# The newer form of attention units from the eighth unit on, with the raw weight tiles in a ring

## The chip, the cores and the metric

The kernel runs on one core of a Trainium2 chip. The metric is the device time of one execution in microseconds (us). Lower is better.

## The reference

A gated linear recurrence over 4 batches, 8 heads, 768 tokens and 48 channels feeds a mixture of 4 experts over 3072 rows of 384. All is float32.

```python
def _attn_ref(q, k, v, alpha):
    state = np.zeros((B, H, D, D)); y = np.zeros_like(q)
    for t in range(S):
        state = alpha[:, :, t, :, None] * state + np.einsum('bhd,bhe->bhde', k[:, :, t], v[:, :, t])
        y[:, :, t] = np.einsum('bhd,bhde->bhe', q[:, :, t], state)
    return y
def _moe_ref(x, domain_probs, w1, w2):       # x: 3072 x 384, w1: 4 x 384 x 1024, w2: 4 x 1024 x 384
    p = domain_probs / (domain_probs.sum(-1, keepdims=True) + 1e-09)
    out = np.zeros((N, D))
    for e in range(E):
        out += p[:, e:e + 1] * (np.maximum(x @ w1[e], 0.0) @ w2[e])
    return out
```

## The kernel before

**Units, groups and tasks.** The tokens are cut into 24 units: a unit `u` is one block of 128 tokens (`cb`, 0 to 5) of one batch (`b`, 0 to 3), with all 8 heads, counted from 0 with the batch running fastest. Units are put into groups `gi`: group 0 has units 0 and 1, group 1 units 2 to 5, group 2 units 6 to 9, and so on; the last has two. A task `(gi, e)` is expert `e` for the tokens of group `gi`: `up` makes 8 tiles of hidden values, each from 9 matmuls (L957, with weights and x split into a rounded part and a rest, three products for three chunks of the contraction) and `down` makes the four sums from 96 matmuls (L1023). ACT writes the rounded hidden value (L959), DVE the rest (`hidden_rest`, L979), both from the PSUM tile `one`. `one` and the sums `ops` share four PSUM banks (tag "g").

**Attention beside the matmuls.** The attention of a group is computed while an earlier group's tasks run: units 6 to 9 during the tasks (1, e), units 10 to 13 during (2, e). `deal` gives every step of a unit a due time on a nominal clock, and `advance` runs the steps that are due between two matmul blocks. So the order of instructions on each engine is fixed when the program is built. Each unit's step ends in a `yield`.

**The older form, `attention`.** DVE turns alpha, k and q into channel rows (L702), and makes the terms of a token with itself (L722, L723). Then for each of seven levels (1, 2, 4, up to 64 tokens) ACT copies q into a zero-padded block (`copy_q`, L756, two copies), DVE scales q and the decays (`next_q`, L763, L765) and the keys (`next_k`, L775, with a copy by ACT, L774). PE makes the scores of six levels as 48 matmuls (L782), with `far` for the seventh (L838), DVE takes them into `near` through masks (L792). The keys are turned on PE (L283, copied by ACT, L894), the results `yps` (L877) and the state terms `sps` (L904) follow.

**The newer form, `in_order`**, is used from unit `in_fours` on. The first two levels are replaced by terms of four tokens in rows: q and alpha are loaded by fours (eight DMAs, L184, into two tiles of raw weights, `four_tiles`, and three, L187, into `row_a`), POOL multiplies them (L492, L494), DVE multiplies by k and reduces (L504, L505). Only levels 2 to 5 are made on PE, as 32 matmuls, with `far`, all at one place (L578, L586). The keys are not turned on PE: DVE transposes them in blocks (L613), and they go to memory and back in another order (`over`, L622, and four DMAs, L629), so that `sps` is 16 small matmuls (L667). The `tail` of a unit (`yps`, L650, and `sps`) runs within the next unit's step. The times of its first 13 steps are HEAD_FIRST for the first such unit, HEAD_SECOND for the second, HEAD_EARLY and HEAD for all others; REST has the others. `load(u + 1, ...)` is issued from unit u's steps.

**Weights.** During group 0, raw float32 pieces of w1 and w2 come from the inputs into `raw` tiles (L232, L236); in the tasks (1, e), w2 still comes raw (four pieces for the next expert at the start of `down`), ACT and DVE split each piece (L250, L252), and POOL's queue stores the split piece to `kept` (L253). From then on pieces are read back from `kept` (L225). There are 12 `raw` tiles, in a pool that hands them out in turn; the newer form takes eight of them by `whole_raw` and by `xTs[LAST]` for its own data.

Of the kernel before, what the change touches and what calls it, by code (L numbers as in the profile page):

```python
# [10 lines left out]
F32 = mybir.dt.float32  # L11
F32R = mybir.dt.float32r
# [8 lines left out]
def kernel(  # L21
# [13 lines left out]
    B, H, S, D = q.shape  # L35
    E, DM, F = moe_w1.shape
    P = 128
    NCB = S // P
    NP = H // 2
# [3 lines left out]
    KC = DM // P  # L43
    FCH = F // P
    NT = B * P
    NQ = 4
    QF = F // NQ
    FPQ = FCH // NQ
    LEVELS = [1 << i for i in range(7)]
    HALF = P // 2  # L50
    FOUR = 4
# [90 lines left out]
    HEAD_SECOND = [0.02, 0.06, 0.1, 0.13, 0.16, 0.2, 0.25, 0.31, 0.37, 0.45, 0.52, 0.61, 0.66]  # L142
    REST = [0.05, 0.17, 0.3, 0.42, 0.58]
    in_runs = 2
    in_fours = half + 2 * B
    MARGIN = 6.0
    waiting = deque()
    clock = 0.0
# [7 lines left out]
    def load(u, names):  # L156
        if u >= len(units):
            return
        cb, b = units[u]
        for nm in names:  # L160
            src = srcs[nm][b, :, cb * P:(cb + 1) * P, :].rearrange("h s d -> s h d")
            if u == in_fours and nm == "q":
                nc.gpsimd.memset(row_a, 1.0)
            if u == in_runs and nm != "v":
                nc.gpsimd.memset(runs_of[nm][:, :, RUN - HD // 4:], 0.0)
            for g in range(P // QUAD if u >= in_runs and nm != "v" else 0):
                i, tail = divmod(g, 2)
                off, n = (QUAD, RUN - HD // 4) if tail else (0, RUN)
                runs = srcs[nm][b].rearrange("(a i) s d -> i a (s d)", i=2)[
                    i, :, cb * P * D:(cb + 1) * P * D].rearrange("a (t n) -> t a n", t=QUAD)  # L170
                nc.sync.dma_start(out=runs_of[nm][QUAD * g:QUAD * (g + 1), :, :n],
                                  in_=runs[:, :, off:off + n])
            if u >= in_runs and nm == "a":
                continue
            if u < in_fours or nm != "q":
                nc.sync.dma_start(out=raw(u, nm)[:, :, :D], in_=src)
                continue
            by_four = lambda t: t[b, :, cb * P:(cb + 1) * P].rearrange("h (t f) d -> t h (f d)", f=FOUR)
            if u == in_fours:
                four_tiles.extend(whole_raw().rearrange("p (h f d) -> p h f d", f=FOUR, d=D) for _ in range(2))  # L180
            fours[u] = four_tiles
            for i, t in enumerate(fours[u]):
                for j in range(FOUR):
                    nc.sync.dma_start(out=t[j::FOUR].rearrange("p h f d -> p h (f d)"),  # L184
                                      in_=by_four(q)[:, H // 2 * i:H // 2 * (i + 1)])
            for j in range(FOUR - 1):
                nc.sync.dma_start(out=row_a[j::FOUR].rearrange("p h f d -> p h (f d)")[:, :, D * j:],  # L187
                                  in_=by_four(alpha)[:, :, D * (j + 1):])
# [13 lines left out]
        return kept[l][expert(gi, e) * NQ + c]  # L202

    AHEAD = 4
    RAW = 3 * NQ

    def parts_of(l):
        return wts.tile([P, 2, KC * QF], F32R, name=f"w{l + 1}", bufs=AHEAD if l == 0 else NQ)
# [4 lines left out]
    def load_piece(l, i, beside=False, held=None):  # L213
        if i >= E * NQ * LAST:
            return
        gi, k = divmod(i, E * NQ)
        at, c = divmod(k, NQ)
        e = expert(gi, at)
        if at == 0 and gi > 0:
            if held is not None:  # L220
                wt[l][i] = held
            return
        if gi > l:
            w = wt[l][i] = parts_of(l)
            nc.sync.dma_start(out=w.bitcast(F32), in_=stored(l, i))  # L225
            return
        if l == 1 and gi == 0 and not beside:
            return
        w = work.tile([P, KC * QF], F32, name="raw", bufs=RAW)
        wt[l][i] = w  # L230
        if l == 0:
            nc.sync.dma_start(  # L232
                out=w.rearrange("p (c f) -> p c f", f=QF),
                in_=moe_w1[e].rearrange("(c p) f -> p c f", p=P)[:, :, c * QF:(c + 1) * QF])
        else:
            nc.sync.dma_start(  # L236
                out=w.rearrange("p (c d) -> p c d", d=DM),
                in_=moe_w2[e].rearrange("(c p) d -> p c d", p=P)[:, c * FPQ:(c + 1) * FPQ])
# [227 lines left out]
        load(2, "v")  # L466
        yield

    def whole_raw():
        return work.tile([P, KC * QF], F32, name="raw", bufs=RAW)  # L470

    def in_order(u):
        cb, b = units[u]
        k = u - in_fours
# [1 line left out]
        if k < 2:  # L476
            AT_of.append(work.tile([P, NP, P], F32, name="AT"))
            QT_of.append(work.tile([P, NP, P], F32, name="QT"))
        elif k == 2:
            for tiles in (AT_of, QT_of):  # L480
                tiles.append(whole_raw()[:, :NP * P].rearrange("p (a n) -> p a n", n=P))
        AT, QT = AT_of[k % 3], QT_of[k % 3]
        rv = values[u % 2]

# [65 lines left out]
            next_k(li)  # L550
            yield
        if k == 0:
            fifth = whole_raw()[:, :NP * P].rearrange("p (a i n) -> p a i n", i=2, n=HALF)
            nc.gpsimd.memset(fifth, 0.0)
            free.append(fifth)
        for li in range(2, 6):
# [51 lines left out]
        if keep:  # L608
            next_k(6)
            if not quads:  # L610
                quads.append(whole_raw()[:, :NP * P])
            by_quad = quads[0].rearrange("x (t a c) -> x t a c", a=NP, c=QUAD)
            nc.vector.transpose(out=by_quad.rearrange("x t a c -> x a t c"),  # L613
                                in_=KTs[-1].rearrange("x a (t n) -> x a t n", n=QUAD))
# [21 lines left out]
        def tail():  # L636
            yps = ps.tile([P, KC, P], F32, name="yps", tag="w")
            strips = [[] for _ in range(P // QUAD)]
            for c in range(KC):
                for j, strip in enumerate(strips):  # L640
                    p, part = divmod(len(strips) * c + j, 3)
                    terms = [(flat_st[:, p, QUAD * part:QUAD * (part + 1)], QT[:, p, :])] if cb > 0 else []
                    for i in range(2):
                        if part != 2 * (1 - i):
                            at = VD * (2 * p + i) + QUAD * part - D * i
                            terms.append((flat_v[:, at:at + QUAD], lat[:, 2 * p + i, :]))
                    strip += [(c, n == 0, n == len(terms) - 1, *term) for n, term in enumerate(terms)]
            for turn in zip(*strips):
                for j, (c, begins, ends, lhsT, rhs) in enumerate(turn):
                    nc.tensor.matmul(yps[QUAD * j:QUAD * (j + 1), c, :], lhsT=lhsT, rhs=rhs,  # L650
                                     start=begins, stop=ends)
            gi, slot = place[cb, b]
            cols = slice(slot * P, (slot + 1) * P)
            if slot == 0 and gi < LAST:
                xTs[gi] = work.tile([P, 2, KC, NT], F32R, name="xT", bufs=2)
            elif slot == 0:
                xTs[gi] = [work.tile([P, KC * QF], F32R, name="raw", bufs=RAW) for _ in range(2)]
            top, low = (x_part(gi, part)[:, :, cols] for part in range(2))
            nc.scalar.copy(out=top, in_=yps)
            nc.vector.tensor_sub(low, yps, top.bitcast(F32))  # L660
            if not keep:
                return lambda: load(u + 2, "v")
            sps = ps.tile([P, NP, D], F32, name="sps", tag="w")
            for p in range(NP):
                for g in range(P // QUAD):
                    at = QUAD * (NP * g + p)
                    nc.tensor.matmul(sps[QUAD * g:QUAD * (g + 1), p],  # L667
                                     lhsT=AT.rearrange("x a n -> x (a n)")[:, at:at + QUAD],
                                     rhs=rv[:, 2 * p + g // 2, :D], start=True, stop=True)

            def update():
                for i in range(2):
                    rows = slice(HD * i, HD * (i + 1))
                    old, add = st[rows, :, i, :], sps[rows]
                    if cb == 0:
                        nc.vector.tensor_copy(out=old, in_=add)
                    else:
                        nc.vector.tensor_mul(old, old, decs[-1][rows].broadcast_to([HD, NP, D]))
                        nc.vector.tensor_add(old, old, add)
                load(u + 2, "v")  # L680

            return update
# [7 lines left out]
    def attention(u):  # L690
# [172 lines left out]
        def result():  # L863
# [20 lines left out]
            if slot == 0 and gi < LAST:  # L884
                xTs[gi] = work.tile([P, 2, KC, NT], F32R, name="xT", bufs=2)
            elif slot == 0:
                xTs[gi] = [work.tile([P, KC * QF], F32R, name="raw", bufs=RAW) for _ in range(2)]
            top, low = (x_part(gi, part)[:, :, cols] for part in range(2))
            nc.scalar.copy(out=top, in_=yps)
            nc.vector.tensor_sub(low, yps, top.bitcast(F32))  # L890
# [326 lines left out]
```

## Time and profile before

| | us |
|---|---|
| median of 3 runs | 988.38 (988.27 to 989.44) |
| the profiled execution | 984.69 |
| its span | 982.9 |
| PE busy | 960.5 (98%) |
| weight loads busy | 859.1 (87%) |
| DVE busy | 602.2 (61%) |
| ACT busy | 382.7 (39%) |
| POOL busy | 107.1 (11%) |

The granted clock of TensorE is full in all stretches. In rows of the timeline, the columns are the start, the length, engine, line, operation, tiles and shapes, the number of instructions (a float32 matmul of the attention counts as two), and in brackets how long the engine was idle before and what released it. In rows of the windows, a window's length comes first, and then for each engine its busy time with the number of its instructions. SPq is the queue of DMA issues of SyncE. The tasks (1, 0) to (1, 3) run from 151 to 318 us of the span, (2, 0) from 318 to 356.

### The profile page before, as it was taken

The numbers are of one execution on the slowest core, as the hardware profiler recorded it, in microseconds if no ns is written. First come the engines' busy times: TensorE is split into PE (matmuls) and PEld (weight loads), VectorE is DVE, ScalarE is ACT, GpSimd is POOL, SyncE is SP. The second block draws the span as 40 slices with busy tenths as digits, with TensorE's granted clock in tenths as the row PEclk, the third lists the DMA queues.
The fourth block names the chain that finished last, engine by engine and source line by source line (L and its number), as shares of the span: only waits on it lengthen the run. The fifth ranks groups of instructions, "written<-read, shape, count | busy, mean of one in ns | idle before, by whom it ended". The sixth has DMA issues, their size and how long they took to land.

```text
span 982.9 us, 20423 instructions
## 1 busy us (share of the span) xinstructions
PE 960.5 (98%) x8168; PEld 859.1 (87%) x8168; DVE 602.2 (61%) x1208; ACT 382.7 (39%) x834; POOL 107.1 (11%) x137
## 2 busy tenths in 40 slices
PE   8998899999999999999999999999999999999998
PEld 7776677988989889899899899898898999999997
DVE  4788878576788958668558577568677312222222
ACT  4767655463543542432433423434334122111111
POOL 2000001000212210110210110210120000000000
PEclk9999999999999999999999999999999999999999
DMA  9798977485964877864667884669782006060601
GB/s 196 261 298 223 302 219 253 157 260 170 313 214 141 251 229 224 303 221 114 194 209 238 284 240 117 186 196 270 243 213 78 34 1 257 1 254 3 242 31 33
DMA packets 171490, 188.56 MB, mean 192 GB/s; under 512 B 80588, under 2 KB 151116, under 8 KB 171396
## 3 DMA queue, kind: packets, MB, share of 16 engines
q1 hardware_dynamic: 164932, 157.41, 53.3%
q0 software_dynamic: 6016, 29.49, 7.9%
q8 instruction: 64, 1.05, 0.4%
q10 hardware_dynamic: 448, 0.36, 0.1%
q14 instruction: 30, 0.25, 0.1%
HBM read 154.71 MB, written 32.51 MB: 190 GB/s over the span
## 4 chain that ended last, share of the span: by engine, by line
PE 81%; DVE 9%; ACT 4%; DMA 3%; issue 2%; SPq 0%; DVEq 0%; POOL 0%; ACTq 0%; POOLq 0%
PE ops L1023 38%; PE one L957 31%; PE sc L578 3%; PE yps L650 2%; ACT qb L756 2%; DVE w L252 1%; PE sc L782 1%; DVE hT L979 1%; PE yps L877 1%; PE one L951 1%; DMA raw<-in_moe_w_dram 1%; DVE near L792 1%; DMA w<-kept 1%; PE tp L283 1%; PE far L586 1%
## 5 line engine op out<-in xcount | busy, mean ns | idle before, releaser
L1023 PE MATMUL ops<-w,hT 128*128 128x384 f32 x2112 | 377.9, 338 | 2.4 <-DVE hT L979 2.3
L1023 PEld LDWEIGHTS ops<-w,hT 128*128 128x128 f32 x2112 | 365.2, 188 | 8.2 <-DVE hT L979 4.1
L957 PE MATMUL one<-xT,w 128*128 128x512 f32 x1440 | 333.2, 390 | 0.1
L957 PEld LDWEIGHTS one<-xT,w 128*128 128x128 f32 x1440 | 269.4, 188 | 56.7 <-DVE hT L979 1.0
L959 ACT ACTIVATE hT<-one 128x512 fp32r<-128x512 f32 (+1 forms) x192 | 108.0, 563 | 315.6 <-PE one L957 315.0
L979 DVE SCALAR_TENSOR_TENSOR hT<-one,hT 128x512 fp32r<-128x512 f32 (+1 forms) x192 | 121.0, 641 | 106.7 <-ACT hT L959 106.6
L1049 DVE SCALAR_TENSOR_TENSOR acc<-ops,p_all,acc 128x384 f32<-128x384 f32 x66 | 38.7, 610 | 87.0 <-PE ops L1023 86.9
L756 ACT COPY qb<-QT 64x256 f32<-64x256 f32 x126 | 51.5, 409 | 33.3 <-DVE QT L763 17.9
L531 DVE TENSOR_TENSOR QT<-QT,AT 128x256 f32<-128x256 f32 x70 | 33.1, 472 | 50.4 <-ACT qb L525 40.0
L492 POOL TENSOR_TENSOR ra<-ra 128x384 f32<-128x384 f32 x28 | 28.7, 1026 | 298.8 <-DMA ra<-in_alpha_dram 297.7
L951 PE MATMUL one<-xT,raw 128*128 128x256 f32 (+1 forms) x240 | 44.9, 340 | 0.4 <-ACT xT L453 0.4
L1058 POOL DMA_DIRECT2D out_dram<-acc x22 | 12.0, 548 | 305.3 <-DVE acc L1049 304.4
L1023 PE MATMUL ops<-raw,hT 128*128 128x384 f32 x128 | 44.9, 493 | 0.0
L253 POOL DMA_DIRECT2D kept<-w x32 | 17.2, 539 | 247.6 <-DVE w L252 120.1
L951 PEld LDWEIGHTS one<-xT,raw 128*128 128x128 f32 x240 | 38.0, 191 | 5.2 <-ACT xT L453 0.6
L763 DVE TENSOR_TENSOR QT<-QT,AT 128x256 f32<-128x256 f32 x60 | 25.3, 421 | 26.2 <-ACT qb L756 25.8
L494 POOL TENSOR_TENSOR raw<-raw,ra 128x576 f32<-128x576 f32 x28 | 40.6, 1470 | 1.1
L957 PE MATMUL one<-raw,w 128*128 128x256 f32 x288 | 35.2, 283 | 0.0
L957 PEld LDWEIGHTS one<-raw,w 128*128 128x128 f32 x288 | 35.1, 192 | 0.0
L1023 PEld LDWEIGHTS ops<-raw,hT 128*128 128x128 f32 x128 | 23.1, 190 | 13.4 <-issue 0.6
L525 ACT COPY qb<-QT 64x256 f32<-64x256 f32 x80 | 32.1, 402 | 7.0 <-DVE QT L531 3.5
L792 DVE COPY_PREDICATED near<-masks,sc 128x256 f32<-128x256 uint8 x54 | 28.8, 533 | 7.2 <-PE sc L782 6.2
(163 smaller groups left out, 957.9 us busy)
## 6 DMA issues: line engine op xcount, KB each, us to landing
w<-kept SPq DMA_DIRECT2D x108, 768.0 KB, 6.1
kept<-w POOLq DMA_DIRECT2D x32, 768.0 KB, 6.8
raw<-in_moe_w_dram SPq DMA_DIRECT2D x44, 384.0 KB, 7.1
raw<-in_q_dram SPq DMA_DIRECT2D x112, 96.0 KB, 2.8
rv<-in_v_dram SPq DMA_DIRECT2D x24, 192.0 KB, 3.8
rk<-in_k_dram SPq DMA_DIRECT2D x22, 192.0 KB, 2.9
out_dram<-acc POOLq DMA_DIRECT2D x22, 192.0 KB, 2.3
sa<-in_alpha_dram SPq DMA_DIRECT2D x44, 88.0 KB, 3.7
```

The source lines that it names most:

```text
L494: nc.gpsimd.tensor_mul(t[:, :, 1:], t[:, :, 1:], row_a[:, H // 2 * i:H // 2 * (i + 1)])
L525: nc.scalar.copy(out=qbs[li][rows, :, i, :].rearrange("p a (b r) -> p a b r", r=m), in_=qv[rows])
L531: nc.vector.tensor_mul(qv, qv, spread(dv[:, :, :, 0], m))
L578: nc.tensor.matmul(banks[li // 2 - 1][HALF * s:HALF * (s + 1), li % 2, 2 * p:2 * p + 2, :], lhsT=KTs[li][:, p, HALF * s:HALF * (s + 1)], r ...
L756: nc.scalar.copy(out=qb[rows, :, i, :].rearrange("p a (b r) -> p a b r", r=m), in_=qv[rows])
L792: nc.vector.copy_predicated(near.rearrange("p a (b two r) -> p a b two r", two=2, r=m)[:, :, :, 1, :], mk.unsqueeze(1).broadcast_to([P, H, ...
L951: nc.tensor.matmul(one, lhsT=w[:, kc], rhs=xTs[gi][:, 0, kc, lo:hi], start=(kc == 0), stop=(kc == KC - 1))
L957: nc.tensor.matmul(one, lhsT=w[:, of_w, kc], rhs=x_part(gi, of_x)[:, kc, :n], start=k == 0, stop=k == len(turns) - 1)
L959: nc.scalar.activation(out=parts[0], in_=one, func=ACT.Relu)
L979: nc.vector.scalar_tensor_tensor(out=low, in0=x, scalar=0.0, in1=top.bitcast(F32), op0=ALU.max, op1=ALU.subtract)
L1023: nc.tensor.matmul(sums[slot], lhsT=h, rhs=w, start=(n == begins[slot]), stop=(n == ends[slot]))
L1049: nc.vector.scalar_tensor_tensor(out=acc, in0=part, scalar=scale, in1=acc, op0=ALU.mult, op1=ALU.add)
```

## The change

`in_fours` goes from 10 to 7: units 7, 8 and 9 are built by `in_order` instead of `attention`. Unit 6 stays in the older form. Units 7 and 8 become the ones with HEAD_FIRST and HEAD_SECOND, and unit 9 onwards use HEAD_EARLY and HEAD. So unit 7's head is dealt into the time of unit 6, in task (1, 0). The 12 raw tiles get names and one buffer each, and stand in a list `raws`: a weight piece takes the tile at its front and puts it back at the end, and `keep=True` takes a tile out for good. In the older pool a tile's buffer is handed out again after 12 further pieces, and w2 pieces are still loaded while units 7 to 9 are computed.

```diff
-    in_fours = half + 2 * B
+    in_fours = half + B + 1
...
-                four_tiles.extend(whole_raw().rearrange("p (h f d) -> p h f d", f=FOUR, d=D) for _ in range(2))
+                four_tiles.extend(whole_raw(keep=True).rearrange("p (h f d) -> p h f d", f=FOUR, d=D) for _ in range(2))
...
     AHEAD = 4
-    RAW = 3 * NQ
+    def raw_tile(i, dtype=F32):
+        return work.tile([P, KC * QF], dtype, name=f"raw{i}", bufs=1)
+
+    raws = deque((i, raw_tile(i)) for i in range(3 * NQ))
+
+    def whole_raw(keep=False):
+        if keep:
+            return raws.popleft()[1]
+        raws.rotate(-1)
+        return raws[-1][1]
...
-        w = work.tile([P, KC * QF], F32, name="raw", bufs=RAW)
+        w = whole_raw()
...
-    def whole_raw():
-        return work.tile([P, KC * QF], F32, name="raw", bufs=RAW)
-
...
-                tiles.append(whole_raw()[:, :NP * P].rearrange("p (a n) -> p a n", n=P))
+                tiles.append(whole_raw(keep=True)[:, :NP * P].rearrange("p (a n) -> p a n", n=P))
...
-            fifth = whole_raw()[:, :NP * P].rearrange("p (a i n) -> p a i n", i=2, n=HALF)
+            fifth = whole_raw(keep=True)[:, :NP * P].rearrange("p (a i n) -> p a i n", i=2, n=HALF)
...
-                quads.append(whole_raw()[:, :NP * P])
+                quads.append(whole_raw(keep=True)[:, :NP * P])
...
-                xTs[gi] = [work.tile([P, KC * QF], F32R, name="raw", bufs=RAW) for _ in range(2)]
+                xTs[gi] = [raw_tile(raws.popleft()[0], F32R) for _ in range(2)]
```

The last edit stands in both `in_order` and `attention`.

## The prediction

> **What bounds the kernel now.** I read the page first, then busy time by task, then PE's timeline, its waits, and the rows of DVE, POOL and SP around the units that the change touches. A task is one `(gi, e)`: 72 up matmuls (L957), 96 down matmuls (L1023), and what attention puts between them. From the page, and then the windows of seven tasks, (1,0) to (1,3) and (2,0) to (2,2) (length, then busy time and instructions of PE, PEld, DVE, ACT, POOL, then clock, DMA share, GB/s):
>
> ```profile
> PE 960.5 (98%) x8168; PEld 859.1 (87%) x8168; DVE 602.2 (61%) x1208; ACT 382.7 (39%) x834; POOL 107.1 (11%) x137
> ```
> ```profile
> 151.19:193.98 42.79, 42.79 (x407) 38.12 (x405) 30.32 (x63) 20.75 (x46) 3.21 (x6) 1.00 0.68 229
> 193.98:234.90 40.92, 40.25 (x342) 36.17 (x341) 26.33 (x54) 19.68 (x41) 2.13 (x4) 1.00 0.74 237
> 234.90:275.25 40.35, 40.24 (x341) 36.17 (x341) 31.34 (x60) 20.81 (x43) 8.47 (x9) 1.00 0.78 259
> 275.25:318.14 42.89, 41.43 (x349) 36.43 (x349) 36.12 (x63) 17.51 (x35) 8.72 (x11) 1.00 0.54 161
> 318.14:356.37 38.23, 37.95 (x329) 34.30 (x329) 32.55 (x65) 15.41 (x34) 6.27 (x6) 1.00 0.70 205
> 356.37:394.05 37.68, 37.68 (x330) 34.35 (x330) 25.10 (x51) 13.91 (x30) 6.22 (x6) 1.00 0.85 258
> 394.05:431.70 37.65, 37.65 (x329) 34.33 (x329) 25.99 (x53) 13.01 (x28) 4.32 (x4) 1.00 0.76 246
> ```
>
> PE is the bound, at full clock. The matmuls of the two layers are the same in all seven, but a task that carries one unit of the old form takes over 40 us and one with the new form 37.68. Where PE does stop in this stretch, DVE is the cause. PE's rows at the end of (1,3)'s up phase, and DVE's of the same moment:
>
> ```profile
> 294.14 1.31 PE L1023 MATMUL ops<-w,hT 128*128 128x384 f32 x6 [0.22 <-DVE hT L979]
> 296.58 1.32 PE L1023 MATMUL ops<-w,hT 128*128 128x384 f32 x6 [1.13 <-DVE hT L979]
> ```
> ```profile
> 293.40 0.68 DVE L979 SCALAR_TENSOR_TENSOR hT<-one,hT 128x512 fp32r<-128x512 f32 x1
> 295.85 0.68 DVE L979 SCALAR_TENSOR_TENSOR hT<-one,hT 128x512 fp32r<-128x512 f32 x1
> ```
>
> PE goes on 0.06 us after an L979 ends. `one` and `ops` share four banks (tag g), and L979 is the last reader of a bank: tile fc+4 cannot start before L979 of tile fc. That is the wait to count, and it applies to the changed program too.
>
> **The PE work.** Start to start on PE's timeline, an old unit costs 2.02 (four products) + 1.52 (`far` and two products) + 0.35 (turning the keys) + 1.66 (`yps`) + 0.81 (`sps`) = 6.36 us; a new one 1.55 + 0.46 + 1.91 + 0.54 = 4.46. Three units change (7, 8, 9): 3 x 1.90 = 5.7 us. The tasks say more, because the old form's pieces break the matmul stream in more places (in (1,2), L957 takes 16.57 us instead of 16.36, L1023 17.42 instead of 16.85) and because the stalls go. In the changed program's PE order, (1,1), (1,2), (1,3) and (2,0) each hold exactly the steady list: 72 + 96 matmuls, one `yps`, one `sps` of 16, four products, one `far`. At 37.68 us each they lose 3.24, 2.67, 5.21 and 0.55, in all 11.67. (1,0) loses four old products of unit 7 (2.01) and takes over the new ones with `far` (309.33 to 311.79, 2.46): +0.45. With no stall anywhere: -11.2 us.
>
> On the 16 small `sps` matmuls: they are 32 records in 0.46 us of PE, 14 ns each. The Trainium skill (TensorE: Matmul & The Clock Gate, section "Wait — 56ns, not 53.3ns?") says that start-to-start never drops below about 25 ns. By that floor the 32 would take 0.8 us and the gain would be 1.0 us less over three units; the trace disagrees, and I keep the row.
>
> **What DVE then does in (1,0).** Here the head of unit 7 (HEAD_FIRST) falls on top of the old unit 6 and of the splitting of w2. DVE's list in program order, with durations start to start from its rows, from 151.68 (the second L1049; unit 7's L488 of a and k, 1.9 us, fit into the 1.88 us that DVE idled ahead of it): L1049 0.54, two L252 1.73, L808 0.60, L504 and L505 1.84, L979 0.60, so tile 0 is done at 157.0; a level of unit 6 0.92, two L792 1.32, L504 and L505 1.84, L979: tile 1 at 161.7; L252 0.87, L488 0.95, L509 0.61, a level 0.90, two L792 0.79, L979: tile 2 at 166.4; L252, a level of unit 7 1.12, L979: tile 3 at 169.0. PE wants to start tile 5 at 163.4, tile 6 at 165.5, tile 7 at 167.5 (2.04 us a tile after 151.19, and 2.02 of products between). Tile 6 waits 0.9, tile 7 0.6 more: 1.5 us even if every operand is there.
>
> Two things come on top. First, L504 reads what POOL's L494 writes, and POOL waits for `ra`. SP ends `sq` of unit 7 at 142.91; then come eight L184 and three L187. How long these take, for the first and for two later units:
>
> ```profile
> 250.67 11.60 SPq L184 DMA_DIRECT2D raw<-in_q_dram  x8
> 320.12 5.66 SPq L184 DMA_DIRECT2D raw<-in_q_dram  x8
> 383.56 5.32 SPq L184 DMA_DIRECT2D raw<-in_q_dram  x8
> ```
>
> The long one ran while the DMA engines were full (share 0.92 in that down phase); from 143 to 155 their share is 0.63, 0.38, 0.00 and 0.16 in steps of 3 us, so I take 6. Then 1.93 for the L187, 1.8 to POOL's start (1.4 to 2.9 in the rows), 2.15 for two L492, 1.45 for the first L494: 156.3, while DVE reaches L504 at 154.6. DVE waits 1.7. Second, POOL slows DVE:
>
> ```profile
> 329.15 2.10 POOL L492 TENSOR_TENSOR ra<-ra 128x384 f32<-128x384 f32 x2 [6.35 <-DMA ra<-in_alpha_dram]
> 331.33 3.18 POOL L494 TENSOR_TENSOR raw<-raw,ra 128x576 f32<-128x576 f32 x2
> ```
> ```profile
> 330.68 0.85 DVE L531 TENSOR_TENSOR QT<-QT,AT 128x256 f32<-128x256 f32 x1 [1.33 <-ACT qb L525]
> 331.57 1.31 DVE L533 TENSOR_TENSOR AT<-AT 128x16 f32<-128x16 f32 x1
> ```
>
> L531 otherwise takes 0.42 and this L533 0.19; with a third one (333.74, 1.06) one batch of POOL costs DVE 2.2 us. A waiting DVE is not slowed, so the two overlap: I take 2.0 together. The L979 are 2.0 later, tile 5 waits 0.3, tile 6 2.6, tile 7 0.6: a stall of 3.5 us (bounds 0 and 14.6, below). (1,0): +0.45 + 3.5 = +3.95.
>
> The Trainium skill (SBUF — State Buffer, "Who interferes with whom") says that a DVE operation with two SBUF inputs and a GpSimd operation that reads SBUF exclude each other, the loser blocked for the whole instruction. The rows agree in kind: L979, one of whose inputs is in PSUM, kept its 0.68 at 333.13. By the rule DVE could lose all of POOL's 5.3 us instead of 2.0, and the sum below would be about -1.6 instead of -4.8.
>
> **The other tasks.** In (1,1), unit 8's head (HEAD_SECOND) meets four L252. The same count from the task's start T: L488 and L596 of units 8 and 7 can only follow `sc` of unit 7, 2.1 us before T; tile 3's L979 ends at T+15.2 where tile 7 wants T+14.3, tile 4's at T+17.6, tile 5's at T+19.1: 1.7 us of stall. DVE's waits for ACT's `qb` copies were 2.0 us in (2,0), the task with this head before; some of that adds. I take 2.3 (1.7 to 3.7): -3.24 + 2.3 = -0.9. In (1,2) and (1,3) DVE has, in the 16.4 us of the up phase, eight L979 (4.8), four L252 (3.5), L596, L545 and L613 (1.8) and four levels (4.0), about 14 us, in an order where every L979 is in time; I give 0.3 each, the stall of (2,0): -2.4 and -4.9. (2,0): -0.55. Nothing later changes.
>
> **Queues, at no cost.** SP carries 8 x 96 + 288 + 512 - 192 = 1376 KB more per unit, 5.8 us at (1,1)'s 237 GB/s: a DMA share of about 0.9, beside 0.85 in a steady task without a stall. The w1 pieces (L225) queue behind it but are needed a task later. L236 now stands behind L629, which waits for `over` (longest 9.7 us in SP's waits): issued at T+22 at worst and 7.1 to landing, needed at T+40. L629 itself must land before `sps` at T+30; by its place behind L184 and `over` I count T+25 to T+28, and without that cover PE stops 1 to 3 us a task. On POOL two L253 and two L1058 go some 4 us later, read by nobody soon. ACT loses about 3 us a unit (four L756, two L774, one L894). The ring hands out the oldest tile, long read when it is asked for: 0.
>
> **Sum.** 3.95 - 0.9 - 2.4 - 4.9 - 0.55 = -4.8 us. The profiled execution took 984.69 (span 982.9 and 1.8 around it), 3.7 below the median of the runs, 988.38; I apply the difference to the median: 983.6.
>
> **The rivals.**
> 1. *DVE keeps up*, total stalls under 3 us: 977.2 to 980.0. For it: in (1,0) before, PE had no stall though the last L979 ended 2.7 us after the up phase. Against: the count. 0.16.
> 2. *The gain is eaten*: DVE loses POOL's whole 5.3 us (3.2 more in (1,0): 986.8), or L629 is late in three tasks by 1 to 3 us (986.6 to 989). 0.13.
> 3. *Slower*: the first L184 and L187 land late and DVE, waiting at L504, holds every L979 behind it. At the worst rows (11.60 for L184, 8.3 to landing for `ra`) the first L494 ends at 167.7 instead of 156.3; tile 4 then waits 8.7, and with tiles 5 to 7 the stall is 14.6: 994.7. The change breaks even at a stall of 8.3, L494 at about 161, and is slower by 0.2% from about 163.5. For it: the same first load took 11.60 before. Against: the DMA engines have room here. 0.09.
>
> The forecast has 0.62. 0.2%, or 2.0 us, is about what a measurement of this kernel can tell from no change; so faster 0.78 (forecast and rival 1), same 0.13, slower 0.09. The range 979.0 to 987.5 leaves out the best of rival 1 and rival 3.
>
> **What would show it.** Right: (1,1) to (2,0) at 37.7 to 40 us, (1,0) at 45 to 47, with waits of PE L957 on DVE L979 in (1,0); PE loses some 5.7 us of matmul work. Wrong: (1,0) over 50 us with DVE waiting on POOL at L504, waits of L667 for a DMA, or stalls over 1 us in (1,2) and (1,3).

## The result and the profile after

The changed kernel is slower by a little: 988.71 us median against 985.43 for the kernel before, 13 runs of each, a ratio of 1.0029 with a 95% interval of 1.0017 to 1.0041. The prediction said 983.6 us and faster, so its sign was wrong. (It started from 988.38, the median of 3 runs before; the 13 runs put that kernel at 985.43.) In the profiled executions the spans are 987.9 and 982.9 us, 5.0 apart where the medians are 3.3 apart; the tasks below are those of the profiled executions.

In the changed kernel's lines, L225 to L253 of before are 9 higher, and those from `in_order` on 6 higher (L979 is L985, L492 and L494 are L498 and L500, L504 and L505 are L510 and L511). The matmul work did go: PE's busy time fell by 5.2 us, where 5.7 were forecast. The first line of its page, to set beside 960.5 us of PE and 107.1 of POOL before:

```profile
PE 955.3 (97%) x8132; PEld 853.9 (86%) x8132; DVE 616.2 (62%) x1211; ACT 373.1 (38%) x813; POOL 123.6 (13%) x149
```

The windows of the tasks (1,0) to (2,0) of the changed kernel (columns as before: length, busy time of PE, PEld, DVE, ACT, POOL, granted clock, DMA share, GB/s):

```profile
151.41:201.23 49.82, 45.29 (x415) 39.65 (x413) 38.80 (x69) 20.09 (x45) 15.34 (x15) 0.97 0.70 227
201.23:244.32 43.09, 38.91 (x329) 34.25 (x329) 37.98 (x68) 17.39 (x35) 7.06 (x8) 1.00 0.86 264
244.32:283.85 39.53, 38.14 (x329) 34.25 (x329) 32.80 (x60) 16.79 (x35) 7.39 (x8) 1.00 0.89 278
283.85:323.50 39.65, 38.22 (x329) 34.44 (x329) 33.78 (x61) 15.68 (x32) 8.53 (x10) 1.00 0.68 203
323.50:361.17 37.67, 37.67 (x329) 34.34 (x329) 25.87 (x50) 14.21 (x31) 7.21 (x8) 1.00 0.68 186
```

Against before these are +7.03, +2.17, -0.82, -3.24 and -0.56 us, in all +4.6; the rest of the span is the same (626.5 and 626.7 us after (2,0)). PE holds 329 matmul records in (1,1) to (2,0), as foretold, but only (2,0) runs at its steady 37.67. The others stop, and (1,0) also shows a clock below 1. PE's waits from 140 to 345 us (total, times, longest):

```profile
PE one L963 <- DVE hT L985: 5.9, 3, 2.5
PE far L592 <- DVE st L684: 2.5, 1, 2.5
PE far L592 <- DVE xT L666: 1.4, 1, 1.4
PE ops L1029 <- DVE hT L985: 1.0, 2, 0.8
PE sps L673 <- DMA AT<-over: 0.6, 1, 0.6
```

The first line is the wait that the prediction counted; most of it lies in (1,0), where it is larger than forecast. The second and third, at `far`, it did not count at all. The first two of the three L963 waits stand at the end of (1,0)'s up phase, on PE's timeline:

```profile
166.31 2.33 PE L963 MATMUL one<-xT,w 128*128 128x512 f32 x9 [1.99 <-DVE hT L985]
171.18 6.00 PE L963 MATMUL one<-xT,w 128*128 128x512 f32 x18 [2.54 <-DVE hT L985]
```

Together PE stops for 4.53 us, where 3.5 were forecast. And the second row has a new thing in it: 18 matmuls, two tiles, take 6.00 us where two tiles take 4.09 in an up phase without a stop (a quarter of 16.36). The windows of 2 us there show why:

```profile
169.00:171.00 2.00, 0.00 (x0) 0.00 (x0) 1.93 (x6) 1.71 (x4) 0.00 (x0) 1.00 0.98 404
171.00:173.00 2.00, 1.82 (x5) 1.44 (x6) 1.97 (x5) 0.00 (x0) 0.47 (x1) 0.58 0.88 249
173.00:175.00 2.00, 2.00 (x7) 1.57 (x6) 1.93 (x7) 0.81 (x2) 0.60 (x2) 0.57 0.89 313
```

The third number from the end is the granted clock. In half-microsecond windows it is 0.50 from about 171.3 to 174.7 us, and 1.00 before and after: the stall was followed by 3.4 us at half clock.

Why L985 was late is in the rows of DVE and POOL at the start of (1,0):

```profile
152.44 2.64 DVE L261 TENSOR_TENSOR w<-raw,w 128x768 fp32r<-128x768 f32 x2
155.00 1.49 DVE L814 TENSOR_TENSOR near<-ident,dot 128x512 f32<-128x512 f32 x1
157.80 2.16 DVE L510 TENSOR_TENSOR raw<-raw,rk 128x768 f32<-128x768 f32 x1 [1.31 <-POOL raw L500]
160.00 0.95 DVE L511 TENSOR_REDUCE dot<-raw 128x16 f32<-128x768 f32 x1
160.87 0.68 DVE L985 SCALAR_TENSOR_TENSOR hT<-one,hT 128x512 fp32r<-128x512 f32 x1
```
```profile
152.63 3.31 POOL L498 TENSOR_TENSOR ra<-ra 128x384 f32<-128x384 f32 x2 [12.67 <-DMA ra<-in_alpha_dram]
156.02 3.13 POOL L500 TENSOR_TENSOR raw<-raw,ra 128x576 f32<-128x576 f32 x2
```

POOL runs from 152.63 to 159.15. In that time every DVE operation with two inputs in SBUF is longer: the two L261 2.64 instead of 1.81, L814 1.49 instead of 0.68, L510 2.16 instead of 0.95. L511, which starts when POOL has ended, has its plain 0.95. With the wait of 1.31 DVE loses 4.1 us ahead of tile 0's L985. POOL is slowed too, its L498 to 3.31 us. The loads were not late: the eight L184 took 5.80 us, where 6 were taken.

### The profile page after: what moved, and what is told of

Read it like the earlier page. It is cut to its first block, busy times and chain, and to the rows that moved or that the text cites. A ratio compares the mean times of both kernels' runs of the same rounds, so it can differ in the third digit from the quotient of the medians.

```text
span 987.9 us, 20418 instructions
## 1 busy us (share of the span) xinstructions
PE 955.3 (97%) x8132; PEld 853.9 (86%) x8132; DVE 616.2 (62%) x1211; ACT 373.1 (38%) x813; POOL 123.6 (13%) x149
## 4 chain that ended last, share of the span: by engine, by line
PE 74%; DVE 11%; DMA 6%; ACT 4%; issue 3%; SPq 1%; POOL 0%; DVEq 0%; ACTq 0%; POOLq 0%
PE ops L1029 34%; PE one L963 31%; PE sc L584 3%; PE yps L656 2%; DMA over<-raw 2%; ACT qb L762 1%; DMA w<-kept 1%; DVE w L261 1%; DMA raw<-in_moe_w_dram 1%; DVE hT L985 1%; PE far L592 1%; DVE near L798 1%; DVE raw L510 1%; DMA AT<-over 1%; PE one L957 1%
## 5 line engine op out<-in xcount | busy, mean ns | idle before, releaser
L1029 PE MATMUL ops<-w,hT 128*128 128x384 f32 x2112 | 375.8, 337 | 1.1 <-DVE hT L985 1.0
L1029 PEld LDWEIGHTS ops<-w,hT 128*128 128x128 f32 x2112 | 365.5, 188 | 6.7 <-issue 3.4
L963 PE MATMUL one<-xT,w 128*128 128x512 f32 x1440 | 334.6, 392 | 5.9 <-DVE hT L985 5.9
L963 PEld LDWEIGHTS one<-xT,w 128*128 128x128 f32 x1440 | 270.6, 188 | 63.8 <-DVE hT L985 7.7
L985 DVE SCALAR_TENSOR_TENSOR hT<-one,hT 128x512 fp32r<-128x512 f32 (+1 forms) x192 | 120.9, 641 | 109.3 <-ACT hT L965 109.3
L537 DVE TENSOR_TENSOR QT<-QT,AT 128x256 f32<-128x256 f32 x84 | 38.8, 462 | 58.5 <-ACT qb L531 35.3
L498 POOL TENSOR_TENSOR ra<-ra 128x384 f32<-128x384 f32 x34 | 36.2, 1064 | 307.1 <-DMA ra<-in_alpha_dram 305.8
L500 POOL TENSOR_TENSOR raw<-raw,ra 128x576 f32<-128x576 f32 x34 | 49.5, 1476 | 1.3
L762 ACT COPY qb<-QT 64x256 f32<-64x256 f32 x84 | 34.3, 409 | 30.3 <-DVE QT L769 20.2
L1029 PE MATMUL ops<-raw,hT 128*128 128x384 f32 x128 | 45.3, 496 | 0.0
L531 ACT COPY qb<-QT 64x256 f32<-64x256 f32 x96 | 38.6, 402 | 13.7 <-DVE QT L537 8.7
L665 ACT CAST xT<-yps 128x384 fp32r<-128x384 f32 x15 | 7.2, 479 | 86.2 <-PE yps L656 86.2
L510 DVE TENSOR_TENSOR raw<-raw,rk 128x768 f32<-128x768 f32 x34 | 34.6, 1018 | 1.8 <-POOL raw L500 1.8
L963 PE MATMUL one<-raw,w 128*128 128x256 f32 x288 | 35.2, 283 | 0.0
L1029 PEld LDWEIGHTS ops<-raw,hT 128*128 128x128 f32 x128 | 23.3, 192 | 13.6 <-issue 0.8
L963 PEld LDWEIGHTS one<-raw,w 128*128 128x128 f32 x288 | 35.1, 192 | 0.0
```

The source lines that it names most:

```text
L498: nc.gpsimd.tensor_mul(row_a[:, :, j], row_a[:, :, j - 1], row_a[:, :, j])
L500: nc.gpsimd.tensor_mul(t[:, :, 1:], t[:, :, 1:], row_a[:, H // 2 * i:H // 2 * (i + 1)])
L510: nc.vector.tensor_mul(t, t, row_k[:, some].unsqueeze(2).broadcast_to([P, H // 2, FOUR, D]))
L531: nc.scalar.copy(out=qbs[li][rows, :, i, :].rearrange("p a (b r) -> p a b r", r=m), in_=qv[rows])
L537: nc.vector.tensor_mul(qv, qv, spread(dv[:, :, :, 0], m))
L762: nc.scalar.copy(out=qb[rows, :, i, :].rearrange("p a (b r) -> p a b r", r=m), in_=qv[rows])
```

## The experiments

The tasks' lengths in the profiled execution of each run, in us, and the ratio of its runs to those of the kernel before, with its 95% interval:

| run | (1,0) | (1,1) | (1,2) | (1,3) | (2,0) | ratio to before |
|---|---|---|---|---|---|---|
| before | 42.79 | 40.92 | 40.35 | 42.89 | 38.23 | 1 |
| changed kernel | 49.82 | 43.09 | 39.53 | 39.65 | 37.67 | 1.0029 (1.0017 to 1.0041) |
| e1_ring | 42.80 | 40.90 | 40.38 | 42.88 | 38.62 | 1.0005 (0.9987 to 1.0022) |
| e2_no_pool | 44.51 | 43.59 | 39.63 | 39.65 | 37.67 | 0.9976 (0.9959 to 0.9993) |
| e3_scratch | 48.62 | 43.49 | 39.61 | 39.63 | 37.68 | 1.0033 (1.0014 to 1.0052) |
| e4_bank | 48.78 | 42.72 | 39.14 | 37.95 | 37.67 | 0.9986 (0.9969 to 1.0002) |
| e5_late | 44.36 | 47.87 | 38.97 | 39.61 | 37.68 | 1.0010 (0.9992 to 1.0027) |
| e6_from8 | 42.79 | 43.50 | 43.27 | 39.65 | 37.67 | 1.0018 (0.9999 to 1.0036) |
| e7_late_bank | 44.31 | 43.31 | 39.70 | 37.95 | 37.67 | 0.9972 (0.9953 to 0.9991) |
| e8_from8_late_bank | 42.79 | 40.84 | 45.79 | 37.93 | 37.68 | 0.9983 (0.9965 to 1.0000) |
| e9_third | 44.85 | 45.06 | 39.48 | 37.94 | 37.67 | 0.9974 (0.9957 to 0.9992) |
| e10_late8 | 44.31 | 39.68 | 52.47 | 37.95 | 37.67 | 1.0067 (1.0047 to 1.0087) |
| e11_bank_third | 49.33 | 42.02 | 39.35 | 37.92 | 37.68 | 1.0003 (0.9983 to 1.0022) |

The theories: (1) POOL's work beside DVE, as a wait and as a slowing, makes the stall of (1,0), and the stall lowers the clock; (2) DVE simply has too many instructions in the up phases of (1,0) and (1,1); (3) the ring or the loads hold something up.

**The ring alone.**

```diff
-    in_fours = half + B + 1
+    in_fours = half + 2 * B
```

> The changed kernel with the new form beginning where it did before (unit 10), so that of the whole change only the ring of raw tiles is left. If the ring costs nothing: the time of the kernel before within 0.2%, tasks (1,0) to (2,0) at 42.8, 40.9, 40.4, 42.9 and 38.2 us within 0.3 each. If the ring's fixed turn makes loads wait (third theory): (1,0) or (1,1) longer by 1 us or more, with PE or ACT waiting for a raw tile.

The tasks are those of before within 0.4 us, the ratio 1.0005. The ring costs nothing; of theory 3 that part falls.

**Without POOL's products of unit 7.**

```diff
-        for j in range(1, FOUR - 1):
+        for j in range(1, FOUR - 1) if k > 0 else ():
             nc.gpsimd.tensor_mul(row_a[:, :, j], row_a[:, :, j - 1], row_a[:, :, j])
-        for i, t in enumerate(fours[u]):
+        for i, t in enumerate(fours[u] if k > 0 else ()):
             nc.gpsimd.tensor_mul(t[:, :, 1:], t[:, :, 1:], ...)
```

> The changed kernel without POOL's products of unit 7 (L498 and L500 of that unit alone; units 8 and later keep theirs), so its output differs. Theory 1 (DVE's wait for POOL and the slowing by it, 4.1 us as read from the rows, are on the path in (1,0), and the stall that they make lowers the clock): the stalls of (1,0) fall from 4.5 us to between 0 and 1.5, the granted clock stays at 1.00 through 165 to 177, (1,0) takes 44 to 45.5 us instead of 49.8; (1,1) to (2,0) stay. Theory 2 (DVE simply has too many instructions in this up phase): (1,0) stays above 47.5. The time falls by 4 to 6 us under theory 1, by less than 2 under theory 2.

(1,0) took 44.51, 5.31 less, PE's stalls there 0.86 us in place of 4.53, the clock 1.00 throughout, PE busy 43.66 in place of 45.29. The window of (1,0), and PE's two waits in it:

```profile
153.53:198.04 44.51, 43.66 (x415) 38.50 (x413) 35.66 (x70) 20.08 (x45) 9.09 (x11) 1.00 0.79 255
```
```profile
169.06 2.33 PE L963 MATMUL one<-xT,w 128*128 128x512 f32 x9 [0.59 <-DVE hT L985]
171.66 2.34 PE L963 MATMUL one<-xT,w 128*128 128x512 f32 x9 [0.27 <-DVE hT L985]
```

DVE's rows of the same work:

```profile
154.56 1.82 DVE L261 TENSOR_TENSOR w<-raw,w 128x768 fp32r<-128x768 f32 x2
156.29 0.69 DVE L814 TENSOR_TENSOR near<-ident,dot 128x512 f32<-128x512 f32 x1
156.89 0.95 DVE L510 TENSOR_TENSOR raw<-raw,rk 128x768 f32<-128x768 f32 x1
```

All three have their plain durations again, and no wait. Theory 1 holds for (1,0), and theory 2, which had (1,0) above 47.5, falls there. Of the 5.31 us, 3.67 are stall and 1.63 the half clock (45.29 - 43.66). The whole time fits: the ratio falls from 1.0029 to 0.9976, about 5 us.

**POOL's work kept, the wait taken away.**

```diff
+            if k == 0:
+                t = whole_raw().rearrange("p (h f d) -> p h f d", f=FOUR, d=D)
             nc.gpsimd.tensor_mul(t[:, :, 1:], t[:, :, 1:], row_a[:, H // 2 * i:H // 2 * (i + 1)])
```

> The changed kernel with L500 of unit 7 working on a tile of the ring that nobody reads for this, in place of the unit's own tiles (the output differs): POOL's work and its time are the same, but DVE's L510 no longer waits for it. It parts the wait (1.3 us) from the slowing (2.8 us). If the two simply add, as I now read the rows: the stall of (1,0) falls by 1 to 1.5 us only, to 3 to 3.5, and (1,0) takes 47 to 48.5, the lowered clock perhaps still there. If the wait was the whole of it: as without POOL, 44 to 45.5. If the slowing takes the wait's place (the two overlap, as the prediction took it): no change, 49.5 to 50.

(1,0) took 48.62, just above the first of the three ranges, and its stalls, 3.06 us, are within that range. But its rows say something else. DVE and then POOL (in this run lines stand 2 higher: L512 is the changed kernel's L510):

```profile
153.19 3.46 DVE L261 TENSOR_TENSOR w<-raw,w 128x768 fp32r<-128x768 f32 x2
156.58 1.90 DVE L816 TENSOR_TENSOR near<-ident,dot 128x512 f32<-128x512 f32 x1
158.41 2.18 DVE L512 TENSOR_TENSOR raw<-raw,rk 128x768 f32<-128x768 f32 x1
```
```profile
153.14 2.70 POOL L498 TENSOR_TENSOR ra<-ra 128x384 f32<-128x384 f32 x2 [12.42 <-DMA ra<-in_alpha_dram]
155.92 3.84 POOL L502 TENSOR_TENSOR raw<-raw,ra 128x576 f32<-128x576 f32 x2
```

The wait is gone and the slowing has grown from 2.8 to 4.1 us (3.46 - 1.82, 1.90 - 0.69, 2.18 - 0.95): DVE loses what it lost before. Tile 0's L987 ended 10.0 us after the task began, against 10.1 in the changed kernel and 5.9 without POOL. So waiting and slowing do take each other's place, my reading that they add falls, and the 1.2 us by which (1,0) is shorter than in the changed kernel are about what that task varies when its head is untouched (48.78 in e4_bank, 49.33 in e11_bank_third, 49.82).

The Trainium skill (SBUF — State Buffer, "Who interferes with whom") says that a DVE operation with two SBUF inputs and a GpSimd operation that reads SBUF shut each other out for the whole instruction. Here the two engines' work, alone, is 4.83 us on POOL (2.08 and 2.75 in e10_late8, where DVE stood still until the last 1.3 us of it) and 3.46 on DVE (the three rows of e2_no_pool), 8.3 in all; together they took 7.45 (153.14 to 160.59). The trace nearly agrees with a full lock.

**`far` in another bank.** `sps` of a unit and `far` of the next share one bank:

```diff
-            sps = ps.tile([P, NP, D], F32, name="sps", tag="w")
+            both = ps.tile([P, NP * D + NP * HALF], F32, name="both", tag="w")
+            shared[u] = both[:, NP * D:].rearrange("p (r s n) -> p r s n", s=2, n=HALF)
+            sps = both[:, :NP * D].rearrange("p (a d) -> p a d", d=D)
...
-        far = ps.tile([P, NP // 2, 2, HALF], F32, name="far", tag="w")
+        far = shared.pop(u - 1, None)
+        if far is None:
+            far = ps.tile([P, NP // 2, 2, HALF], F32, name="far", tag="w")
```

> The changed kernel with `far` of a new unit placed in the same PSUM bank as `sps` of the unit before it (they need 1792 of 2048 bytes a partition), so that `far` no longer waits for the bank of `yps`, which L666 frees late. If PE's waits at L592 (2.49 in (1,1), 1.44 in (1,3)) are real losses of the path: they vanish, (1,1) falls from 43.1 to 40.6 to 41.2 and (1,3) from 39.65 to 38.2 to 38.8, the time by 3 to 4 us. If DVE's backlog is the cause and the bank only its first victim: the next `ops` waits for its L1055 instead and 1 to 2.5 us of the two stay. (1,0) stays at 49 to 50.

(1,3) went from 39.65 to 37.95, its wait at `far` gone: there the bank was the cause. (1,1) gained 0.37 only. Its `far` (L595, the changed kernel's L592), in the row of PE,

```profile
239.42 0.66 PE L595 MATMUL both<-qb,KT 128*64 128x128 f32 x8 [1.27 <-issue]
```

still starts 1.27 us late, and the trace names no releaser; 0.64 more is a wait of `sps` for the DMA from `over`. The same `far` starts 0.5 to 1.4 us late without a releaser in e7_late_bank, e9_third and e11_bank_third, and in e10_late8 it starts 1.0 us after the operation named as its releaser. So in (1,1) the bank was not all that held it, and what else does is not shown by a run. The traces point at one thing. The page lists a DMA queue for instructions:

```profile
q8 instruction: 64, 1.05, 0.4%
```

These are 64 packets, one in 15 us, beside some 16450 instructions of PE and its weight loads, about 256 a packet. In the 13 traces PE has 18 gaps over 0.35 us (after the first 3 us) that no semaphore explains, and every one of them ends 1.3 to 1.7 us after such a packet has landed; here it landed at 237.67. PE was then probably waiting for its instructions. No run tests it.

**Unit 7's L510 and L511 after its level 3**, in the down phase of (1,0); nothing is left out:

```diff
-        for i, t in enumerate(fours.pop(u)):
-            ...
-        load(u + 1, "k")
+        def own_terms():
+            for i, t in enumerate(fours.pop(u)):
+                ...
+            load(u + 1, "k")
+        if k > 0:
+            yield from own_terms()
...
             next_k(li)
             yield
+            if k == 0 and li == 3:
+                yield from own_terms()
+                load(u + 1, "q")
...
-    HEAD_FIRST = [*(0.06 * j for j in range(1, 8)), 0.5, 0.58, 0.66, 0.74, 0.82, 0.93]
+    HEAD_FIRST = [0.06, 0.12, 0.2, 0.27, 0.34, 0.43, 0.52, 0.61, 0.66, 0.71, 0.78, 0.85, 0.93]
```

> The changed kernel with one thing moved: for unit 7 alone the two halves of L510 and L511 (and with them the loads of unit 8's k and q) come after level 3, in the down phase of (1,0), in place of the up phase; the times in HEAD_FIRST follow. Nothing is left out. DVE has idle time there (it was idle for some 9 us between 176 and 201 in the changed kernel). Theory 1 (POOL's wait and slowing together with these halves hold L985): 3.8 us of DVE and the 1.3 us of waiting leave the up phase, the slowing of L261 and L814 stays; stalls 0 to 1 instead of 4.5, granted clock 1.00, (1,0) 43.7 to 44.8. Theory 2 (too many instructions whatever they are): the same sign, but the levels that now come earlier fill the place, (1,0) 45.5 to 47.5. Later loads for unit 8 may cost 0 to 1.5 in (1,1).

(1,0): 44.36, with stalls of 0.40 and 0.21 and the clock at 1.00, as theory 1 said. But (1,1) grew to 47.87: the loads for unit 8 come later with the moved lines, POOL starts at 193.62 in place of 180.79, and now unit 8's L511 (the changed kernel's L510) waits 2.42 us for it and is slowed to 2.18 at the head of (1,1)'s up phase. The stalls there are 2.12, 0.26 and 1.39 us, `far` waits 2.10, and the clock is halved after that from 237.6 to 241.0 us. The collision moved one task on; I had given it 0 to 1.5 us.

**The newer form from unit 8 on** (`in_fours = half + B + 2`), so that two units change.

> The changed kernel with the new form beginning one unit later (unit 8), so that HEAD_FIRST falls in (1,1) and not in (1,0), where w2's pieces are still split beside it. Theory 1 and 2 alike: (1,0) returns to 42.8. In (1,1) the head of the first new unit meets an up phase with 4 L261 but without the two extra pieces of (1,0), and POOL works in it: if its L510 waits or is slowed as in (1,0), (1,1) is 43 to 46 with a lowered clock; if the lighter phase takes it, 41 to 42.5. (1,2) 39 to 40, (1,3) 39 to 40, (2,0) 37.7. Sum against before -1 to -5.

(1,0) is as before. (1,1) is 43.50 with a stall of 2.39 and (1,2) 43.27, more than expected: `sps` waits 2.17 us for `over` there. The time is that of before within the interval or a little above it. So the first head stalls (1,1) too, by 2.39 without a lowered clock where (1,0) had 4.53 and a lowered clock; but against the changed kernel it gains one unit's matmuls less and loses 3.74 us in (1,2).

**Both changes together.**

> The changed kernel with both: the halves of L510 and L511 of unit 7 after level 3, and `far` in the bank of `sps`. If the gains add: (1,0) 43.7 to 44.8, (1,1) 41.5 to 43, (1,2) 39.1, (1,3) 38.0, (2,0) 37.7; 8 to 9 us less than the changed kernel in the profiled tasks, a ratio to the kernel before of 0.992 to 0.996.

The gains add in (1,0) and (1,3), but the whole gains less than expected. (1,1) is 43.31, with stalls of 0.92 and 1.43 in the up phase: unit 8's POOL again starts late, at 193.31. The ratio, 0.9972, is about 2.8 us less than the kernel before, with an interval below 1, and the changed kernel's interval lies above 1: this version beats both.

> As the last, with the new form beginning at unit 8: one unit fewer gains 1.9 us of matmul work, but (1,0) stays at 42.8. (1,1) 41.3 to 43 (head of the first new unit, its L510 late), (1,2) 38 to 40, (1,3) 38.0, (2,0) 37.7; against the kernel before -4 to -8 us, a ratio of 0.992 to 0.997. If it beats the version that begins at unit 7, the place of the first head in (1,0) costs more than a unit's matmuls bring.

From unit 8 on, (1,0) and (1,1) are at the old values, and the collision stands in (1,2): L512 there (the changed kernel's L510) waits 3.22 us for POOL and is slowed to 2.18, a stall of 3.32 follows, 45.79. It is not shown to beat the version that begins with unit 7 (0.9983 against 0.9972, with intervals that overlap).

**Unit 9's head later, unit 8's L510 and L511 later.** Three versions with the shared bank. The first adds to the two changes together:

```diff
+    HEAD_THIRD = [0.8, 0.88, 0.03, 0.07, 0.12, 0.17, 0.25, 0.34, 0.43, 0.52, 0.6, 0.66, 0.7]
...
+                        early, near_by = (HEAD_EARLY, HEAD) if u > in_fours + 2 else (HEAD_THIRD[:2], HEAD_THIRD[2:])
```

> The version with late halves and the shared bank, and in addition the head of unit 9 moved out of the down phase of (1,1): only its first two steps stay there, L510, L511, L515 and the levels 0 and 1 (about 8 us of DVE) go behind the burst of unit 8 and into (1,2). If DVE has simply too much in (1,1), a whole head of unit 8 and more than half of unit 9's: (1,1) falls from 43.3 to 40.5 to 42 (the stalls of its up phase, 2.6 us, stay), (1,2) is 39.5 to 41. If (1,1) is held by its up phase alone: (1,1) 42.5 to 43.3 and (1,2) up to 1 us longer, no gain.

The second of the three treats unit 8 as unit 7 was treated:

```diff
-        if k > 0:
+        if k > 1:
             yield from own_terms()
...
-            if k == 0 and li == 3:
+            if k < 2 and li == 3:
...
-    HEAD_SECOND = [0.02, 0.06, 0.1, 0.13, 0.16, 0.2, 0.25, 0.31, 0.37, 0.45, 0.52, 0.61, 0.66]
+    HEAD_SECOND = [0.02, 0.06, 0.1, 0.14, 0.2, 0.27, 0.34, 0.58, 0.62, 0.66, 0.7, 0.74, 0.78]
```

> As the last, and unit 8's L510 and L511 too come after its level 3, in the down phase of (1,1). If they and POOL's products beside them make the stalls of 1 to 2.6 us in that up phase: (1,1) 38.5 to 40, (1,2) 39 to 41 with unit 9's loads later (its POOL and L510 may then collide with the up phase of (1,2), as unit 8's did in (1,1) when unit 7's halves were moved: 41 to 43). Against the kernel before: a ratio of 0.990 to 0.997.

The third has no late halves at all:

> The shared bank and the moved head of unit 9 without the late halves of unit 7. (1,0) as in the changed kernel, 48.5 to 50, with the lowered clock; (1,1) 40 to 41.5, since its loads for unit 8 come early again; (1,2) 39 to 41. It says what of (1,1)'s length in the version with late halves comes from the loads that the late halves hold up (1 to 2 us if they matter).

In e9_third (1,1) did not fall: 45.06, with 5 us less DVE work in it (35.55 busy), and a stall of 2.76 in its up phase. In e11_bank_third, where unit 8's loads are early again, it was 42.02 with DVE only 31.94 busy. So how much DVE has to do in the task as a whole is not what holds (1,1): theory 2 falls in that form. The ratio of e9_third, 0.9974, is that of e7_late_bank.

In e10_late8 the up phase of (1,1) has no stall left, and the task is 39.68; what it has over the PE time of 37.92 is the 1.76 at `far`. Unit 9's later head alone did not do this, so unit 8's L510 and L511 in that phase, with the steps of HEAD_SECOND that moved with them, made its stalls. In the changed kernel they ran there at their plain 0.95 (from 201.24), so there it is their own time and not POOL's that stalls it. Theory 2 holds for (1,1) in this form, that of the place. The bill comes in (1,2). DVE's and POOL's rows (L513 is the changed kernel's L510), and then PE's:

```profile
242.57 2.13 DVE L513 TENSOR_TENSOR raw<-raw,rk 128x768 f32<-128x768 f32 x1 [11.87 <-POOL raw L502]
```
```profile
238.98 2.08 POOL L500 TENSOR_TENSOR ra<-ra 128x384 f32<-128x384 f32 x2 [25.41 <-DMA ra<-in_alpha_dram]
241.14 2.75 POOL L502 TENSOR_TENSOR raw<-raw,ra 128x576 f32<-128x576 f32 x2
```
```profile
250.51 2.08 PE L977 MATMUL one<-xT,w 128*128 128x512 f32 x4 [10.71 <-DVE acc L1069]
```

Unit 9's loads were issued late, DVE stood 11.87 us at the unit's first product with everything else queued behind it, PE stood 10.71 and then ran at half clock until 256.0 us. This is the mechanism of the prediction's third rival, in another task.

## Why the prediction was wrong

By its own steps, in the order of its sum (the tasks came out 9.4 us above it, -4.8 against +4.6):

- **The matmul work and the steady task.** Right. PE's busy time fell by 5.2 us in spite of the half clock, the records in (1,1) to (2,0) are 329, (2,0) is 37.67 (forecast -0.55, came -0.56).
- **(1,0), the count of DVE.** Near: 1.5 us of stall was counted without POOL, and without POOL 0.86 was measured.
- **(1,0), "I take 2.0 together".** This step failed. It was right in kind, a waiting DVE is not slowed and the two overlap, but mis-sized: 4.1 us, seen twice. I took the 2.2 of one batch in a later unit, where DVE had few operations with two inputs beside POOL. In (1,0) four of them stand one behind the other for all of POOL's run, and POOL itself is slowed, 6.4 us in place of 4.8, so that the first L500 ended near 157.8 and not at 156.3. POOL's share of the stall was 3.67 us (4.53 - 0.86). The Trainium skill's rule on the lock (SBUF — State Buffer, "Who interferes with whom"), with which the prediction had DVE lose all of POOL's 5.3 us, was nearer to the 4.1 than the rows that I kept.
- **(1,0), the clock.** No step had it, 1.63 us. "PE is the bound, at full clock" was read off seven tasks of the kernel before, in which PE never stopped for more than 1.13 us. That the clock was full in all stretches was not so: the same profile has it at 0.50 from 17.1 to 20.5 us, after a gap of 1.43, and a mean of 0.998. How much a stall costs in clock was in part luck (see the last section). (1,0) came to +7.03 in place of +3.95: 1.03 more stall, 1.63 of clock, and 0.42 by which 43.66 without stalls is above the estimated 43.24.
- **(1,1), the up phase.** Right: from 201.23 to the first L1029 at 219.87 is 18.64 us, 2.28 above the 16.36 of the matmuls; 2.3 was taken. Of it 1.60 stand in the rows as waits for L985.
- **(1,1) and (1,3), `far`.** "`one` and `ops` share four banks ... That is the wait to count" was too narrow. `far` takes the bank that `yps` leaves (tag "w", two banks), L666 on DVE frees it, and L666 stands behind the next unit's head. In (1,3) this was 1.44, given back in full (-1.70). In (1,1) the wait was 2.49, but sharing the bank gave back 0.37 only: L666 had ended at 239.62, and `far` began at 240.50. The rest is the wait without a releaser of e4_bank, which no step had. With it (1,1) came to +2.17 in place of -0.9, and (1,3) to -3.24 in place of -4.9.
- **(1,2), "0.3 each".** Came 0.80 at L1029 behind L985 and 0.60 at `sps` for the DMA from `over`: -0.82 in place of -2.4. L635 was issued at 266.3 and landed at 276, the price of 1 to 3 us that the prediction named under "queues, at no cost".
- **The ring at no cost.** Right (e1_ring). The loads of unit 7 on time: right.
- **The rivals.** None came as written. Rival 2 had two of the causes, nearly all of POOL's time and a late L629, but put the result at 989 at most and alike or better than before. (By its own prices, 1 to 3 us in three tasks, it reaches 992.6 and not 989.) That 988.71 lies within its figures is luck, for they start from the 988.38. The third's place and cause (late loads) were wrong for this change, and e10_late8 shows the mechanism where loads are late. The signs I counted on as "wrong" did show: waits at `sps` for a DMA, and stalls over 1 us in (1,3).

## What to carry to other kernels

When work is moved to an in-order engine in the middle of a phase that it feeds, count per place, not per task: who else reads the same memory then (an idle second engine that starts up beside it slows both), and every buffer that this engine frees, the small ones too, since each is a wait of the bound engine. Price a stall of TensorE above its length, for the clock may fall behind it. And where a step is moved, the loads behind it move too: three of the versions only carried the collision one task on.

## What the runs showed of the hardware

**The clock falls after short gaps, and where a gap lies decides.** A stall of 1.84 us was enough (e3_scratch):

```profile
166.92 3.91 PE L965 MATMUL one<-xT,w 128*128 128x512 f32 x9 [1.84 <-DVE hT L987]
```

The clock was 0.50 from 167.1 to 170.5. In the changed kernel it came after the second of two gaps (1.99, then 2.54), in e4_bank after one of 1.98, and in e5_late after one of 2.10. Each of these four halvings lasted 3.4 us, at exactly half. A gap of 2.39 (e6_from8), one of 2.76 (e9_third) and one of 3.32 (e8_from8_late_bank) were not followed by it. The Trainium skill (TensorE: Matmul & The Clock Gate, "What's actually happening") describes two rates, full and half, set by a free-running window of about 3.4 us. The trace agrees on the half and on the 3.4.

The traces show the window, too. Within a trace the halvings start whole multiples of 3.413 us apart: at 120.11 and 171.31 in the changed kernel (15 of them), at 16.90, 33.97 and 167.08 in e3_scratch (5 and 39). Cut into such windows from 125 to 975 us, every window in which PE was idle for 1.84 us or more is followed by half clock (1.84, 1.98, 2.10 and 2.54 in the four runs above), and none with 1.83 or less is: 1.83 in the changed kernel's window of the first gap, 1.79 and 1.53 in the two that share the 3.32, 1.71 in the fuller one of the two that share the 2.39. So a little over half a window idle was enough, and whether a gap falls into one window or is cut in two is luck. Earlier than 125 us, where PE has many small matmuls, windows with less were followed too (1.79 in the changed kernel, ahead of 120.11).

**POOL is slowed by DVE as well.** The two L498 took 3.31 us beside L261 and L814, and 2.08 beside a waiting DVE.
